# Pooled attention with a gated feed-forward block: weight words joined by VectorE, another product order in the scores, more movable operations, a new schedule

## The chip, the core and the metric

The kernel runs on one core of a Trainium2 chip. The metric is the device time of one launch in microseconds (us). TensorE (PE) multiplies, VectorE (DVE), ScalarE (ACT) and GpSimd (POOL) do the elementwise work, and SyncE (SP) issues the transfers.

## What is computed

```
q_pool = q.reshape(B, H, S // 2, 2, D).mean(axis=3)          # B,H,S,D = 4,8,1152,64
scores = (q_pool @ k.T) / sqrt(D)                            # 576 queries x 1152 keys
attn   = exp(scores - max);  attn /= attn.sum() + 1e-9
x      = (attn @ v), heads side by side                      # 4 x 576 x 512
h      = relu(x @ w_in)                                      # 512 -> 1024
c[s]   = conv_w[0]*h[s-1] + conv_w[1]*h[s] + conv_w[2]*h[s+1]
out    = (h * sigmoid(c)) @ w_out                            # 1024 -> 512
```

Everything is float32 outside; the three weights arrive as float64 and are put together from their 32-bit words on the chip.

## The kernel before

**Stages.** The 32 heads are worked in 16 pairs of two. Per pair the pooled queries stand in five blocks `d` of up to 128 rows (the last one holds 64 rows of each head and counts as one unit), so there are nine score units per pair and 144 in all. A unit is: three products into three PSUM banks (`scores`, L459: main 0 is 512 keys on the head's own half of the rows, main 1 512 keys on the other half with the turned queries `qd`, main 2 the 128 keys that are left), the row maximum by DVE (`top`, L471), the exponential by ACT (`expo`, L476, which also sums), the inverse of the sum (L489 or L493, then L499), and then the weights are split into two half-precision parts: `high` (L523 on ACT or L518 on POOL) and `low` (L526, DVE), which a transposing transfer (L539) turns. For seven heads (`X32`) there is no split: the rows are scaled (`norm`, L557 on ACT, L561 on POOL or DVE), turned by TensorE (L575) and copied out of PSUM by ACT (L580). There are two PSUM buffers for scores (`r_s`), so that the scores of a unit wait for the exponential of the unit two before.

After the units of a group of blocks come the values (`values`, L605 and L611), a copy out (L621), and another split (`high` L627 on ACT or L629 on POOL, `low` L634 on DVE). After four pairs, one batch, comes the feed-forward block: `feed` runs eight chunks of 128 columns, each a product of twelve matmuls (L695), a relu (L701, ACT), the first tap (`tap0`, L708 on ACT or L712 on POOL), two more taps (L719, DVE), a tanh (L725, ACT) and the gate (L729, DVE); `second` is the last product (L902 on split parts for three of the groups, else L908 and L914), copied out by ACT and stored.

**Weights.** Each of 17 blocks of weights passes through ACT `size` (L991), DVE `clamp` (L995), three DVE bit operations (L1004, L1009, L1013), ACT `rest` (L1019, which turns the low words into numbers), a DVE product (L1026) and an addition (L1028, DVE or POOL). The queries' two rows are summed by L303 and copied and turned by ACT (L306, L310).

**Order.** Every operation is a task with an engine, and some have an alternative engine (`alt`). Three tables at the head of the file say all: `ORDER` is the order in which the tasks are issued, `SWAPPED` names the tasks that run on their alternative, `SLOTS` gives every tile its buffer. Each engine works its own tasks strictly in that order; what it waits for are the results of the others.

## Time and profile before

| | us |
|---|---|
| median of the runs shown | 636.63 (636.33 to 636.86) |
| span of the profiled execution | 633.9 |
| TensorE busy | 583.3 |
| VectorE busy | 575.9 |
| ScalarE busy | 520.2 |
| GpSimd busy | 159.6 |

The span runs from the first to the last instruction of the profiled execution; 2.7 us of the median lie around it. Busy times are unions of the instructions' records. Records of one engine overlap by some hundredths of a microsecond, so that a sum of durations is a little larger than the union. A wait is named as "engine line <- what ended it".

### The profile page before, as it was taken

To read this page: it belongs to the slowest core of one execution; us is meant where nothing else is said; L and a number is where in the kernel's file an instruction comes from. 1 tells how busy PE (TensorE), PEld (TensorE's weight loads), DVE (VectorE), ACT (ScalarE), POOL (GpSimd) and SP (SyncE) were. 2 spreads that over 40 slices of the span, in tenths; PEclk is the share of its full clock that TensorE was granted. 3 is DMA by queue.
4 is the path that set the end of the run, shared out by engine and by line. 5 is a ranking of instruction groups with operands and counts; after the bars stand their busy time and mean duration, and the time that the engine had idled before them with its cause. 6 is when DMAs were issued, how large, how long until landed. Compare 5 with 4: busy or idle time off the path is not lost. (4 is left out here: it accounts for less than half of the span.)

```text
span 633.9 us, 11947 instructions
## 1 busy us (share of the span) xinstructions
PE 583.3 (92%) x4427; PEld 365.1 (58%) x4427; DVE 575.9 (91%) x948; ACT 520.2 (82%) x976; POOL 159.6 (25%) x166
## 2 busy tenths in 40 slices
PE   5679887898999899999999999999998999999997
PEld 3346554566665556546666666475665646566853
DVE  4999989999999999989998999999999999997771
ACT  5999989989998897879977899787869985775761
POOL 0332436533233312210212511202330122322210
PEclk7869989999999999999999999999999999999999
DMA  7788975847975599998989998999999898887601
GB/s 246 234 221 223 197 127 118 207 116 191 182 197 109 131 193 169 177 219 162 248 176 190 177 241 168 159 217 195 199 181 210 175 173 152 166 153 152 93 35 42
DMA packets 277386, 109.63 MB, mean 173 GB/s; under 512 B 264912, under 2 KB 266192, under 8 KB 277328
## 3 DMA queue, kind: packets, MB, share of 16 engines
q1 hardware_dynamic: 277328, 108.87, 83.3%
q8 instruction: 35, 0.57, 0.4%
q14 instruction: 23, 0.19, 0.1%
HBM read 37.77 MB, written 4.72 MB: 67 GB/s over the span
## 5 line engine op out<-in xcount | busy, mean ns | idle before, releaser
L476 ACT ACTIVATE p<-s,sm 128x1152 f32<-128x1152 f32 x144 | 175.2, 1217 | 41.2 <-DVE sm L471 18.8
L459 PE MATMUL s<-kt,qt 64*128 64x512 f32 (+3 forms) x704 | 189.0, 484 | 20.7 <-ACT p L476 16.5
L471 DVE TENSOR_REDUCE sm<-s 128x1 f32<-128x1152 f32 x144 | 193.1, 1348 | 7.3 <-PE s L459 6.9
L526 DVE SCALAR_TENSOR_TENSOR hl<-p,sm,hl 128x1152 f16<-128x1152 f32 (+1 forms) x116 | 167.0, 1449 | 4.3 <-POOL hl L518 2.4
L459 PEld LDWEIGHTS s<-kt,qt 64*128 64x128 f32 (+1 forms) x704 | 92.6, 178 | 124.3 <-issue 78.1
L459 PE MATMUL s<-kt,qd 64*128 64x512 f32 x256 | 147.3, 658 | 0.0
L518 POOL TENSOR_SCALAR hl<-p,sm 128x1152 f16<-128x1152 f32 (+1 forms) x52 | 72.1, 1388 | 230.1 <-DVE sm L499 145.8
L605 PE MATMUL a<-pt,v 128*64 128x256 f16 (+2 forms) x1566 | 119.8, 272 | 0.4 <-DVE v L399 0.4
L695 PE MATMUL a<-x,wi 128*128 128x257 f16 (+3 forms) x864 | 105.4, 274 | 3.6 <-ACT h L701 1.7
L605 PEld LDWEIGHTS <-v 128*64 128x64 f16 x1566 | 91.1, 110 | 10.2 <-issue 2.2
L695 PEld LDWEIGHTS <-wi 128*128 128x128 f16 x864 | 76.6, 98 | 30.3 <-issue 10.6
L523 ACT ACTIVATE hl<-p,sm 128x1152 f16<-128x1152 f32 (+1 forms) x64 | 79.4, 1249 | 12.3 <-DVE sm L499 9.1
L908 PE MATMUL a<-wo,g 128*128 128x512 f32 x160 | 74.7, 604 | 0.0
L719 DVE SCALAR_TENSOR_TENSOR g<-h,cw,g 128x255 f32<-128x255 f32 (+3 forms) x144 | 66.7, 482 | 4.1 <-ACT g L708 2.5
L575 PE MATMUL a<-ident,p 128*128 128x128 f32 (+1 forms) x315 | 49.1, 281 | 17.1 <-ACT pt L580 7.3
L611 PE MATMUL a<-pt,v 128*64 128x256 f32 (+1 forms) x252 | 64.1, 409 | 0.0
L575 PEld LDWEIGHTS a<-ident,p 128*128 128x128 f32 (+1 forms) x315 | 32.9, 144 | 31.1 <-ACT pt L580 10.1
L580 ACT ACTIVATE pt<-a 128x384 f32<-128x384 f32 (+2 forms) x98 | 44.6, 475 | 5.3 <-PE a L575 5.2
L701 ACT ACTIVATE h<-a,bs 128x257 f32<-128x257 f32 (+3 forms) x72 | 33.9, 472 | 14.3 <-PE a L695 9.4
L561 POOL TENSOR_SCALAR p<-p,sm 128x1152 f32<-128x1152 f32 (+1 forms) x20 | 28.1, 1408 | 69.0 <-DVE sm L499 42.9
L908 PEld LDWEIGHTS a<-wo,g 128*128 128x128 f32 x160 | 28.4, 190 | 28.8 <-issue 26.9
L611 PEld LDWEIGHTS a<-pt,v 128*64 128x64 f32 x252 | 33.4, 137 | 10.3 <-issue 0.7
(135 smaller groups left out, 648.8 us busy)
## 6 DMA issues: line engine op xcount, KB each, us to landing
qin<-in_q_dram SPq DMA_DIRECT2D x15, 640.0 KB, 4.6
kt<-in_k_dram SPq DMA_DIRECT2D x15, 576.0 KB, 5.0
vin<-in_v_dram SPq DMA_DIRECT2D x9, 576.0 KB, 4.4
g<-in_moe_w_in_dram SPq DMA_DIRECT2D x8, 512.0 KB, 4.6
w<-in_moe_w_out_dram SPq DMA_DIRECT2D x8, 512.0 KB, 4.2
out_dram<-o SPq DMA_DIRECT2D x16, 256.0 KB, 2.6
vin<-in_v_dram SPq DMA_DIRECT2D x7, 288.0 KB, 3.9
v<-in_v_dram SPq DMA_DIRECT2D x7, 288.0 KB, 4.1
```

The lines of the kernel that those rows point to most:

```text
L459: nc.tensor.matmul(out=w, lhsT=f, rhs=kk, start=True, stop=True)
L471: nc.vector.tensor_reduce(out=sm[:, e:e + 1], in_=runs(st[e]), axis=AX.XY, op=ALU.max, negate=True)
L476: nc.scalar.activation(out=p.tile().rearrange("p (a n) -> p a n", a=2), in_=runs(st[e]), func=AF.Exp, bias=sm[:, e:e + 1], scale=1.0, accu ...
L518: eng.tensor_scalar(out=hl[rows, 0], in0=ps_[e][rows], scalar1=sm[rows, 6 + e:7 + e], scalar2=1.0, op0=ALU.mult, op1=ALU.mult,)
L523: nc.scalar.activation(out=hl[rows, 0], in_=ps_[e][rows], func=AF.Copy, scale=sm[rows, 6 + e:7 + e])
L526: nc.vector.scalar_tensor_tensor(out=hl[rows, 1], in0=ps_[e][rows], scalar=sm[rows, 6 + e:7 + e], in1=hl[rows, 0], op0=ALU.mult, op1=ALU.s ...
L575: nc.tensor.transpose(w[:, (i - a1) * nq:(i - a1 + 1) * nq], ps_[e][rows, i * P:(i + 1) * P], ident[rows, rows])
L605: nc.tensor.matmul(out=to, lhsT=o.v[:, e, c, vc:vc + D], rhs=o.pt[y, e][:, hl * NC + c, 0:n], start=(c == 0 and j == 0), stop=(c == NC - 1 ...
L611: nc.tensor.matmul(out=to, lhsT=o.v[:, e, c].bitcast(F32), rhs=p32.rearrange("p (a n) -> p a n", a=NC)[:, c, 0:n], start=(c == 0), stop=(c ...
L695: nc.tensor.matmul(out=w[:, 0:n], lhsT=wi[:, a, j, f * P:(f + 1) * P], rhs=x.x[:, c, s0:s0 + n], start=(i == 0 and j == 0), stop=(i == 2 a ...
L719: nc.vector.scalar_tensor_tensor(out=c, in0=h[:, t:t + tok], scalar=cw[:, f, t:t + 1], in1=c, op0=ALU.mult, op1=ALU.add)
L908: nc.tensor.matmul(out=w.tile(), lhsT=g[f // 4][:, f % 4, c:c + P], rhs=wo[:, f, :], start=(f == 0), stop=(f == FC - 1),)
```

## The change

The products of a score unit are issued in the order main 2, main 1, main 0. `rest` is gone, and the product behind it reads the low words itself. Five kinds of tasks can now run on another engine: turning the queries, the copies L580 and L621 and the relu on DVE, the clamp on POOL. `ORDER`, `SLOTS` and `SWAPPED` are new (`SWAPPED` has 308 tasks instead of 176); some costs written beside tasks are other numbers, which are used for nothing at run time, and some tags are added.

```diff
         def scores(ends):
-            for main in (0, 1, 2):
+            for main in (2, 1, 0):
                 for e in ends:
...
-        def rest():
-            _, lo32, hi32, mm, a = parts()
-            nc.scalar.activation(
-                out=hi32.bitcast(F32), in_=lo32.bitcast(U32), func=AF.Copy, scale=2.0 ** -52
-            )
-
         def join(n, eng=None):
             _, lo32, hi32, mm, a = parts()
             if n == 0:
-                nc.vector.tensor_tensor(out=mm, in0=mm, in1=hi32.bitcast(F32), op=ALU.mult)
+                nc.vector.scalar_tensor_tensor(
+                    out=mm, in0=lo32.bitcast(U32), scalar=2.0 ** -52, in1=mm, op0=ALU.mult, op1=ALU.mult
+                )
...
-        def clamp():
+        def clamp(eng):
             _, lo32, hi32, mm, a = parts()
-            nc.vector.tensor_scalar(
-                out=mm, in0=mm, scalar1=F64_MIN, scalar2=F64_MAX, op0=ALU.max, op1=ALU.min
+            eng.tensor_scalar(
+                out=mm, in0=mm, scalar1=F64_MAX, scalar2=F64_MIN, op0=ALU.min, op1=ALU.max
             )
...
-        t = add("DVE", 0.08 + m / 1900.0, clamp, after=[t], uses=[tmp], port=True)
+        t = add("DVE", 0.08 + m / 1900.0, clamp, after=[t], uses=[tmp], port=True,
+                alt=("POOL", 0.15 + m / 1113.0, True))
...
-        t = add("ACT", act(m, 0.08), rest, after=[t], uses=both)
...
-        def turn_q(e, cols):
+        def turn_q(eng, e, cols):
             h, g = slice(D - D * e, P - D * e), slice(D * e, D * e + D)
+            if eng is not nc.scalar:
+                eng.tensor_scalar(
+                    out=o.qd.tile()[h, cols], in0=o.qin[g, 0, cols], scalar1=QSCALE, scalar2=1.0,
+                    op0=ALU.mult, op1=ALU.mult,
+                )
+                return
...
+                        if eng is nc.scalar:
+                            nc.scalar.activation(out=to, in_=src, func=AF.Copy)
+                        else:
+                            eng.tensor_copy(out=to, in_=src)
...
                         add("ACT", act((a2 - a1) * nq), keep, after=[t],
-                            uses=[w, pt])
+                            uses=[w, pt], alt=("DVE", 0.06 + (a2 - a1) * nq / 930.0, False))
...
-        t = add("ACT", act(n, 0.1), keep, after=[t] + o.one, uses=[w] + ([] if all(o.x32) else [o.vs]), takes=[xf])
+        t = add("ACT", act(n, 0.1), keep, after=[t] + o.one, uses=[w] + ([] if all(o.x32) else [o.vs]), takes=[xf],
+                alt=("DVE", dve(n) + 0.01, False))
...
-            t = add("ACT", act(n, 0.155 if halved else 0.085), relu, after=[t, xs[0].back], uses=[w, xs[0].bs], takes=[h])
+            t = add("ACT", act(n, 0.155 if halved else 0.085), relu, after=[t, xs[0].back], uses=[w, xs[0].bs], takes=[h],
+                    alt=None if halved else ("DVE", dve(n) + 0.01, False))
...
 ORDER = """
-hZcZcXaac1c4c0c5c6c7cYh0auc2bNc3abacaddcaededdc8afdbh3h1daagdfahc9h2dtaih4aviiajawh5aEaxdsaybOilh6h7azifijh8aA
...
+hIdXcIcGaacNcJcPcOcQcHashJcKabcRhKaccUcScMcThMadhLaecLafathNh1dbauaghOavahawh4aihPaxc0aBhQcVhYh2hRcWcZhZhUc1hV
...
```

What the tables do is seen in the order of each engine. How many tasks of a kind run where, before and after, is this:

| line before: task | engine | before | after |
|---|---|---|---|
| L995 clamp | DVE / POOL | 17 / 0 | 3 / 14 |
| L303 sum of queries | DVE / POOL | 15 / 3 | 3 / 15 |
| L561 norm (L557 on ACT) | DVE / POOL / ACT | 9 / 20 / 6 | 1 / 23 / 11 |
| L1028 addition | DVE / POOL | 9 / 8 | 5 / 12 |
| L493, L489 sum of a unit | DVE / ACT | 39 / 41 | 23 / 57 |
| L523, L518 high | ACT / POOL | 64 / 52 | 44 / 72 |
| L708, L712 first tap | ACT / POOL | 51 / 21 | 5 / 67 |
| L627, L629 high of x | ACT / POOL | 25 / 11 | 2 / 34 |
| L580 copy of a turned block | ACT / DVE | 98 / 0 | 85 / 13 |
| L310 turning queries | ACT / DVE | 36 / 0 | 29 / 7 |
| L701 relu | ACT / DVE | 72 / 0 | 65 / 7 |
| L621 copy of values | ACT / DVE | 36 / 0 | 33 / 3 |
| L1019 rest | ACT | 17 | 0 |

DVE at the start of the program, up to the first row maximum (L471 before, L480 after; L1029, L1034, L1038 are the bit operations L1004, L1009, L1013, and L304 and L312 sum and turn queries). Before:

```order
L995 TENSOR_SCALAR g<-g 128x512
L1004 TENSOR_SCALAR wo<-g 128x512
L303 TENSOR_TENSOR qin<-qin 128x384
L1009 SCALAR_TENSOR_TENSOR wo<-g,wo 128x512
L303 TENSOR_TENSOR qin<-qin 128x128
L1013 TENSOR_SCALAR g<-wo 128x512
L471 TENSOR_REDUCE sm<-s 128x1
L1026 TENSOR_TENSOR g<-g 128x512
```

After:

```order
L304 TENSOR_TENSOR qin<-qin 128x128
L312 TENSOR_SCALAR qd<-qin 64x128 x2
L304 TENSOR_TENSOR qin<-qin 128x128
L480 TENSOR_REDUCE sm<-s 128x1
L1029 TENSOR_SCALAR wo<-g 128x512
L1034 SCALAR_TENSOR_TENSOR wo<-g,wo 128x512
L1038 TENSOR_SCALAR g<-wo 128x512
L480 TENSOR_REDUCE sm<-s 128x1
```

The first row maximum has moved ahead of all weight work; before, four operations on weights stood in front of it.

PE at its last score units (L459 before, L467 after; L605 is a product with values, L902, after L927, a product of `second`). Before:

```order
L459 MATMUL s<-kt,qt 64x512 x4
L459 MATMUL s<-kt,qt 64x2x64 x2
L459 MATMUL s<-kt,qt 64x512 x4
L459 MATMUL s<-kt,qt 64x2x64 x2
L605 LDWEIGHTS v
L605 MATMUL a<-pt,v 64x256
```

After:

```order
L619 LDWEIGHTS v
L619 MATMUL a<-pt,v 64x256
L467 MATMUL s<-kt,qt 64x2x64 x2
L467 MATMUL s<-kt,qt 64x512 x4
L927 LDWEIGHTS kt
L927 MATMUL a<-w,kt 128x512
```

One product with values of 256 rows (54 matmuls) and three feed chunks of 257 columns (36 matmuls of L695) have moved from behind the last score to ahead of it; the other 570 matmuls behind it are the same.

POOL in the middle of the program (L518 before and L528 after are `high` of a unit, L712 and L736 first taps, L629 and L647 `high` of x). Before:

```order
L712 TENSOR_SCALAR g<-h,cw 128x255
L391 TENSOR_SCALAR v<-vin,vs 128x9x64
L561 TENSOR_SCALAR p<-p,sm 128x1152
L712 TENSOR_SCALAR g<-h,cw 128x321
L518 TENSOR_SCALAR hl<-p,sm 128x1152
L303 TENSOR_TENSOR qin<-qin 128x640
```

After:

```order
L528 TENSOR_SCALAR hl<-p,sm 128x1152 x2
L736 TENSOR_SCALAR g<-h,cw 128x255 x3
L528 TENSOR_SCALAR hl<-p,sm 128x1152
L736 TENSOR_SCALAR g<-h,cw 128x255 x2
L647 TENSOR_SCALAR x<-xf,bs 128x320
L736 TENSOR_SCALAR g<-h,cw 128x255
L304 TENSOR_TENSOR qin<-qin 128x640
```

The same kinds stand there, but almost twice as many of them in all.

## Rows read from the trace of the kernel before

**Rows 1.** Page part 1: busy us, share of span, instructions, by engine.

```profile
PE 583.3 (92%) x4427; PEld 365.1 (58%) x4427; DVE 575.9 (91%) x948; ACT 520.2 (82%) x976; POOL 159.6 (25%) x166
```

**Rows 2.** Busy us by stretch: PE, PEld, DVE, ACT, POOL; granted clock, DMA share, GB/s.

```profile
16.00:128.00 112.00, 91.37 (x587) 56.51 (x585) 106.24 (x179) 106.07 (x206) 45.78 (x42) 0.91 0.80 189
128.00:256.00 128.00, 119.44 (x911) 78.50 (x908) 125.12 (x195) 114.81 (x213) 34.15 (x33) 1.00 0.75 162
384.00:512.00 128.00, 123.76 (x944) 75.85 (x941) 123.21 (x189) 106.88 (x192) 22.40 (x25) 1.00 1.00 190
576.00:634.00 58.00, 53.07 (x583) 34.05 (x580) 34.70 (x98) 30.23 (x83) 7.89 (x11) 0.99 0.34 70
```

**Rows 3.** Waits: engine, line, waited for: us in total, times, longest.

```profile
ACT p L476 <- DVE sm L471: 18.8, 19, 3.2
...
PE s L459 <- ACT p L476: 16.5, 21, 1.6
```

**Rows 4.** Start, by time: start us, us, engine, line, [idle before <- what ended it].

```profile
8.45 0.43 DVE L995 TENSOR_SCALAR g<-g 128x512 f32<-128x512 f32 x1 [7.59 <-ACT g L991]
...
9.99 1.22 PE L459 MATMUL s<-kt,qt 64*128 64x512 f32 x1 [3.69 <-DMA kt<-in_k_dram]
...
10.87 1.35 DVE L471 TENSOR_REDUCE sm<-s 128x1 f32<-128x1152 f32 x1
```

**Rows 5.** DVE groups by form: count | busy us, mean ns | idle before.

```profile
L471 DVE TENSOR_REDUCE sm<-s 128x1 f32<-128x1152 f32 x144 | 193.1, 1348 | 7.3 <-PE s L459 6.9
...
L303 DVE TENSOR_TENSOR qin<-qin 128x640 f32<-128x640 f32 x13 | 10.6, 818 | 0.2 <-DMA qin<-in_q_dram 0.2
...
L561 DVE TENSOR_SCALAR p<-p,sm 128x1152 f32<-128x1152 f32 x5 | 4.1, 811 | 0.0
...
L995 DVE TENSOR_SCALAR g<-g 128x512 f32<-128x512 f32 x8 | 3.4, 421 | 8.1 <-ACT g L991 8.1
```

**Rows 6.** ACT groups by form: count | busy us, mean ns | idle before.

```profile
L523 ACT ACTIVATE hl<-p,sm 128x1152 f16<-128x1152 f32 x60 | 74.4, 1250 | 12.2 <-DVE sm L499 9.1 <-DMA pt<-hl 0.8 <-ACT g L708 0.7
...
L1019 ACT ACTIVATE w<-w 128x512 f32<-128x512 uint32 x8 | 5.4, 681 | 0.0
```

**Rows 7.** POOL by line: durations ns min/median/max, first and last start, forms.

```profile
L518 POOL TENSOR_SCALAR hl<-p,sm x52: 1223/1228/2507, 25.8 to 581.4; 128x1152 f16<-128x1152 f32 x49, 64x1152 f16<-64x1152 f32 x3
...
L712 POOL TENSOR_SCALAR g<-h,cw x21: 486/636/1540, 160.0 to 613.5; 128x255 f32<-128x255 f32 x13, 128x321 f32<-128x321 f32 x4, 128x256 f32<-128x256 f32 x3, 128x65 f32<-128x65 f32 x1
...
L303 POOL TENSOR_TENSOR qin<-qin x3: 456/1547/1722, 3.5 to 199.6; 128x640 f32<-128x640 f32 x2, 128x128 f32<-128x128 f32 x1
```

**Rows 8.** Middle, by time, DVE and then POOL: start us, us, what.

```profile
300.34 1.35 DVE L471 TENSOR_REDUCE sm<-s 128x1 f32<-128x1152 f32 x1
...
311.25 1.41 DVE L526 SCALAR_TENSOR_TENSOR hl<-p,sm,hl 128x1152 f16<-128x1152 f32 x1
...
300.29 1.23 POOL L518 TENSOR_SCALAR hl<-p,sm 128x1152 f16<-128x1152 f32 x1 [11.28 <-issue]
311.32 2.08 POOL L629 TENSOR_SCALAR x<-xf,bs 128x320 f16<-128x320 f32 x1 [9.79 <-ACT xf L621]
```

**Rows 9.** DVE low halves: the group's mean, and min/median/max.

```profile
L526 DVE SCALAR_TENSOR_TENSOR hl<-p,sm,hl 128x1152 f16<-128x1152 f32 x109 | 157.2, 1451 | 4.2 <-POOL hl L518 2.4 <-ACT hl L523 1.2
...
L526 DVE SCALAR_TENSOR_TENSOR hl<-p,sm,hl x116: 1399/1411/2699, 18.3 to 583.0; 128x1152 f16<-128x1152 f32 x109, 64x1152 f16<-64x1152 f32 x7
```

**Rows 10.** Chain that ended last, from 560 us: start us, us, what.

```profile
565.91 3.07 PE a L605 x54
...
571.67 1.32 PE a L695 x12
...
630.10 0.38 ACT o L928
```

**Rows 11.** The same chain: one score unit alone, and two in a row.

```profile
491.37 1.34 PE s L459 x6
...
422.60 2.14 PE s L459 x10
```

More of the change, by code (lines that the diff above doesn't have):

```diff
@@ L160 @@
+JPJRJTKuKBKIKPKWK3LaLhLsLwLDLKLRLYL5McMjMsMuMxMyMFMMMTMZM0M6M7NeNl
 """
@@ L319, in loads @@
             ready = [tq] + [
-                add("ACT", act(turned.stop - turned.start, 0.16), lambda e=e, turned=turned: turn_q(e, turned), after=[t],
-                    uses=[o.qin] + ([o.qd] if e or i else []), takes=[] if e or i else [o.qd]) for e in range(2)
+                add("ACT", act(turned.stop - turned.start, 0.16), lambda eng, e=e, turned=turned: turn_q(eng, e, turned), after=[t],
+                    uses=[o.qin] + ([o.qd] if e or i else []), takes=[] if e or i else [o.qd],
+                    alt=("DVE", 0.08 + (turned.stop - turned.start) / 1900.0, True)) for e in range(2)
             ]
@@ L466, in softmax @@
         for e in range(n):
+            plan.tag = ('softmax', o.pr, d, 2 if m else e)
             p = Buf(r_p)
@@ L550, in softmax @@
                     continue
+                plan.tag = ('softmax', o.pr, d, h)
                 pt = o.pt[y, h]
@@ L564, in norm @@
                     )
-                td = add("POOL", 1.28, norm, after=[iv], uses=[sm, ps_[e]] + ([] if new else [pt]),
+                td = add("POOL", 1.22, norm, after=[iv], uses=[sm, ps_[e]] + ([] if new else [pt]),
                          takes=[pt] if new else [], port=True,
-                         alt=("ACT", act(S, 0.1), False) if d % 2 else ("DVE", 0.08 + S / 1900.0, True))
+                         alt=("ACT", act(S, 0.1), False) if d % 2 else ("DVE", 0.12 + S / 1900.0, True))
                 groups = ((0, 5), (5, 9)) if m else ((0, 3), (3, 6), (6, 9))
@@ L618, in values, with keep @@
         to = slice(1 + first, 1 + first + n)
[L620 to L623 removed]
+        def keep(eng):
+            by = 2.0 ** -14 if all(o.x32) else o.vs[:, 4:5]
+            if eng is not nc.scalar:
+                eng.tensor_scalar(
+                    out=xf[:, 0:n], in0=w[:, 0:n], scalar1=by, scalar2=1.0, op0=ALU.mult, op1=ALU.mult
+                )
+                return
+            nc.scalar.activation(out=xf[:, 0:n], in_=w[:, 0:n], func=AF.Copy, scale=by)
         def high(eng):
@@ L698, in mm, with relu @@
                         )
-            def relu(f=f, w=w, h=h):
+            def relu(eng=nc.scalar, f=f, w=w, h=h):
+                if eng is not nc.scalar:
+                    eng.tensor_scalar(
+                        out=h[:, 0:n], in0=w[:, 0:n], scalar1=xs[0].bs[:, 3:4], scalar2=0.0, op0=ALU.mult, op1=ALU.max
+                    )
+                    return
                 nc.scalar.activation(
```

140 lines of the change are left out of this document (69 added, 71 removed).

## The prediction

> **What bounds the kernel now.** I read the busy times first [rows 1]: TensorE 583.3 us and VectorE 575.9 us of a span of 633.9 us. Neither fills it, so the stretches come next [rows 2], and there the reader is to see that the bound is not one engine. From 16 to 128 us DVE is busy 106.24 and ACT 106.07 of 112 us, and PE only 91.37: the weights are joined there beside the first softmaxes. From 128 to 256 DVE has 125.12 of 128. From 384 to 512 DVE (123.21) and PE (123.76) are level, and the transfers are busy all the time (1.00). From 576 on PE has 53.07 of 58 and DVE 34.70. So DVE sets the pace until the last softmax, shared with ACT at first and with PE later, and what is left then is a tail of matmuls. The waits agree [rows 3]: ACT's exponential waits 18.8 us for DVE's row maximum, and TensorE's scores 16.5 us for the exponential that frees their PSUM buffer. Third, the chain that ended last [rows 10]: from 565.9 us, where the last score unit ends, it is TensorE without a gap worth the name, until the last copy out at 630.1.
>
> The time is therefore made of two pieces: when the last score unit runs, which hangs on DVE's order up to the third-last row maximum (two score buffers), and the matmuls behind that unit.
>
> **DVE's work.** Removed, with durations of [rows 5]: 14 clamps x 0.42 = 5.9 us (16 of 512 columns, one small one, 3 stay); 13 query sums of 640 columns x 0.82, less one of 128 more at 0.29, = 10.4; 8 scalings at 0.81 or a little more = 6.5 to 7.5; four additions of 512 columns at 0.69 (the sum of 640 at 818 ns, less 128 columns at 1.04 ns, the slope between the rows of 640 and of 1152) = 2.7; 16 sums of two columns at 0.15 (the row maximum's 1348 ns less 1152 x 1.04) = 2.5. Together about 28.5. Added: 13 copies of turned blocks from PSUM, 7 relus, 3 copies of values, 7 query turns. DVE copies nothing out of PSUM in this trace; the nearest row is the row maximum, 1152 PSUM columns in 1348 ns, which gives 0.5 us for 384 columns, and I take that (bounds 0.4, as if in SBUF, to 0.6): 13 x 0.5 + 7 x 0.35 + 3 x 0.3 + 7 x 0.35 = 12.3. The joining product keeps its price: two inputs of 512 columns before and after; that it now reads unsigned words has no row of its own on DVE, and ACT's row for that conversion, 681 ns [rows 6], is no longer than DVE's two-input pass, so 0, bounds -1 to +3 us for all 17. Net over the program: -16.
>
> What counts is what stands ahead of the third-last row maximum. Going through both orders with these durations: 27.6 us of the removals and 11.2 of the additions lie ahead of it, and 4.3 us that stood behind it have been moved ahead of it (five taps, two gates, two low halves of x, one of a unit, less one long split). That is -12.1, with 18 instructions fewer; since records overlap by 0.07 us or so, -10.9.
>
> **The start.** DVE's first row maximum starts at 10.87 us [rows 4], though its scores were done at 9.99 - 3.69 = 6.30: in DVE's order four weight operations stand ahead of it, the first of which waits for ACT until 8.45. In the new order only the sums and turns of the first queries are ahead. The first maximum can start some 4 us sooner; the second one needs the second part of the keys, which landed at 9.99 and is issued one transfer (0.6 us) earlier. I take 3 us for DVE (bounds 1 to 4.4).
>
> **ACT.** It loses 17 `rest` at 0.68 [rows 6] = 11.5, 20 high halves at 1.25 = 25, 46 first taps and 23 high halves of x at about 0.5 = 35, and some 11 more: from 520 to about 437. In the first 256 us it was as full as DVE, so this must accompany DVE's relief there, or that would be worth nothing. By itself I give it 2 us (bounds 0 to 6): exponentials that stand behind other ACT work come sooner.
>
> **POOL, and the wait that is added.** All this goes to POOL. With undisturbed times, the minima of [rows 7]: 20 more halves x 1.23 = 24.6, three scalings 3.7, 12 query sums x 1.55 = 20.7 less a short one, 46 taps x 0.5 = 23, 23 halves of x x 0.5 = 12, 14 clamps at 0.7 (between 0.49 for 255 columns and 1.23 for 1152) = 9.8, others 14: 108 us on top of some 137 (159.6 as recorded, with waits in it). An engine that is busy 40% is no bound by itself. But [rows 8] show what it costs: a POOL half of a unit beside a row maximum takes 1.23; a POOL operation on 320 columns that starts with DVE's 1.41 us low half takes 2.08, where short operations take 0.49 undisturbed. POOL waited for DVE. The other way round, [rows 9] have DVE's low halves at 1451 ns on average, 1411 in the median and up to 2699: 109 x 0.04 = 4.4 us lost; they are 167 of some 358 us of DVE's two-input and fast work (575.9 less 193 of maxima and 25 of tiny operations), so in all between 4.4 and 9.4, I take 7.5. Queued behind such an operation are the row maxima, and behind these the exponentials and the scores. Scaled by POOL's work (245 / 137) this grows by 6 us; scaled by its square, by 16. Nothing excludes less, if the order puts POOL beside the maxima, which take 193 us; I take +6, bounds 0 and 16.
>
> If POOL could run beside none of that DVE work, 358 - 26 + 245 = 577 us would have to follow one another in some 617; before, 358 + 137 = 495 in 634. It fits, but with little room, which is the first rival below.
>
> The Trainium skill (SBUF — State Buffer, "Who interferes with whom") gives the rule: DVE and GpSimd share one port pair under an exclusive lock, an operation with two SBUF inputs or in a two-port mode holds it for its whole length, and a reduction never needs it. It speaks against this change, and the trace agrees: 2.08 us against 1.23 beside a maximum. By the rule the sum just made would be a hard floor, 577 us, under the forecast; so the rule alone changes the chance of the rival and not the sum.
>
> **128 keys first.** A unit alone takes 1.34 us on TensorE, two in a row 2.14 [rows 11]. The columns on each half of the rows are the same in either order, so I take 0. Bounds: the short product first may hide a weight load of 0.1 us per unit or expose one more: -13 to +13 over 128 units, of which only those count where TensorE is the bound.
>
> **The tail.** Ahead of the last score now stand one product with values (54 matmuls, 3.07 us in [rows 10]) and three feed chunks (3 x 1.32 to 1.43): 7.1 us less behind it. TensorE must have done these 7.1 us earlier, beside DVE's work; it idles 50.6 us in the span, nearly all before 576, so there is room.
>
> **The sum**, against the execution profiled: 633.9 - 10.9 (DVE) - 3 (start) - 2 (ACT) + 6 (POOL in DVE's way) + 0 - 7.1 (tail) = 616.9. With the 2.7 us that lie between span and median (636.6 - 633.9): 619.6, say **620 us**. Its own range, with start, POOL and ACT at their bounds but not all on one side: 611 to 630.
>
> **Rivals.**
> *POOL and DVE in each other's way.* For: the two together fill 94% of the span by the sum above, and DVE's two-input operations often stand back to back. Against: before, POOL's 137 us cost DVE only 7.5 (5%). If 20% of POOL's 245 us comes back as DVE waiting, that is 49 instead of 7.5, and the time is 636.6 - 16 - 7.1 + 41.5 - 0 = 655; at 14% it is 640. It decides from 12% on (30 us), where the gain is gone: slower.
> *TensorE and the transfers hold the middle.* From 384 to 512 us PE is at 97% and the transfers at 1.00 [rows 2]; DVE's relief there buys nothing. Then of the 10.9 only the 5.8 before 128 us count: 636.6 - 5.8 - 3 + 3 - 7.1 = 627.
> *More than the sum.* ACT is no longer full beside DVE. If half of TensorE's 50 us of idle time goes instead of a third, and the stretch at the lower clock at the start shrinks (0.91 granted from 16 to 128, between the levels of 1.2 and 2.4 GHz), then 606.
> *The score order costs.* If each unit gets 0.1 us longer where TensorE is the bound, the forecast turns to 633.
>
> **How the numbers follow.** The forecast 0.50, POOL against DVE 0.17, the held middle 0.15, more than the sum 0.13, the score order 0.05. A measurement of this kernel can tell 0.2% from no change, here 635.3 to 637.9. Faster: 0.49 + 0.15 + 0.13 + 0.02 = 0.79; within: 0.04, from the score order and the light end of the first rival; slower: 0.17. The range must leave out no more than 2 in 10: 604 leaves out part of the fourth case, about 0.05, and 639 most of the first rival, about 0.14.
>
> **What would show it.** After, DVE busy should be near 560 and ACT near 440, POOL 270 to 330 as recorded, with the median of its halves still 1.23. The first row maximum should start at 6.5 to 7.5 us, the last score unit end at 554 to 562 (565.9 now), and the chain behind it hold 57 us of TensorE. The mean of DVE's low halves tells the first rival: 1.45 to 1.50 us by the forecast, 1.65 and more if POOL is in the way. Two units in a row on TensorE should stay at 2.14. I am wrong in mechanism if the last score unit is not earlier although DVE's work ahead of it shrank; then DVE's idle time tells whether it waits for POOL's results, which would be a wait that I have priced at nothing.

## The result, and the profile after

The changed kernel takes **641.39 us** (median of 14 runs, 637.14 to 646.84), the kernel before 636.53 in the same comparison: ratio 1.0078, interval 1.0058 to 1.0097. It is **0.8% slower**, where 2.6% faster was forecast. The profiled execution has a span of 639.9 us, against 633.9 before. TensorE's granted clock does not make the difference. At the same mean clock over a whole run, 0.976 (a mean between its levels of 1.2 and 2.4 GHz), the runs on record of the kernel before take 636.3 to 638.3 us and those of the changed kernel 639.7 to 644.3. Within the runs of the changed kernel the time does go with the clock (637.1 and 639.9 us at 0.981, 645.0 at 0.970); what drives what there is not shown.

Page part 1 of the changed kernel (busy us, share of the span, instructions), and under it the busy us by stretch, as in [rows 1, 2]:

```profile
PE 582.2 (91%) x4427; PEld 353.5 (55%) x4427; DVE 590.3 (92%) x924; ACT 450.0 (70%) x853; POOL 275.8 (43%) x296
```

```profile
16.00:128.00 112.00, 92.57 (x615) 55.50 (x615) 108.63 (x172) 105.00 (x197) 47.88 (x50) 0.91 0.83 191
128.00:256.00 128.00, 119.24 (x883) 73.84 (x879) 122.82 (x185) 104.92 (x190) 58.76 (x59) 0.97 0.77 165
384.00:512.00 128.00, 118.10 (x881) 69.76 (x882) 120.28 (x180) 75.77 (x145) 53.78 (x54) 1.00 0.92 177
576.00:640.00 64.00, 57.09 (x598) 34.62 (x592) 42.78 (x106) 24.00 (x59) 19.49 (x32) 1.00 0.44 85
```

ACT was relieved by 70 us, and POOL took 116 us more. But DVE, which lost 24 instructions and was to lose 16 us, is busy **14.4 us longer**. Where that time sits is seen in DVE's groups by form (columns as in [rows 5]), and in the low halves' minimum, median and maximum:

```profile
L480 DVE TENSOR_REDUCE sm<-s 128x1 f32<-128x1152 f32 x144 | 192.0, 1345 | 7.2 <-PE s L467 6.6
L536 DVE SCALAR_TENSOR_TENSOR hl<-p,sm,hl 128x1152 f16<-128x1152 f32 x109 | 166.1, 1532 | 4.6 <-POOL hl L528 3.7 <-ACT hl L533 0.2
L743 DVE SCALAR_TENSOR_TENSOR g<-h,cw,g 128x255 f32<-128x255 f32 x64 | 32.8, 534 | 0.6 <-ACT g L732 0.5
L652 DVE SCALAR_TENSOR_TENSOR x<-xf,bs,x 128x256 f16<-128x256 f32 x20 | 13.4, 670 | 2.0 <-POOL x L647 2.0
...
L536 DVE SCALAR_TENSOR_TENSOR hl<-p,sm,hl x116: 1398/1409/2743, 17.1 to 598.4; 128x1152 f16<-128x1152 f32 x109, 64x1152 f16<-64x1152 f32 x7
```

The row maxima (L480, 1345 ns) are as they were (1348 in [rows 5]). The low halves have the same median (1409, and 1411 in [rows 9]) and a mean that rose from 1451 to 1532: most are untouched, and some are twice as long. One such place, by time, DVE and POOL:

```profile
320.96 2.85 POOL L528 TENSOR_SCALAR hl<-p,sm 128x1152 f16<-128x1152 f32 x2 [6.16 <-DVE sm L508]
...
321.56 1.36 DVE L480 TENSOR_REDUCE sm<-s 128x1 f32<-128x1152 f32 x1
322.83 2.18 DVE L536 SCALAR_TENSOR_TENSOR hl<-p,sm,hl 128x1152 f16<-128x1152 f32 x1
```

POOL makes two halves in a row. The row maximum beside the first takes its usual 1.36 us. The low half at 322.83 starts while POOL is in its second half, and takes 2.18 instead of 1.41.

**A count over all records.** For each form at each line of DVE I took the duration at the lower quarter as undisturbed, and added up what instructions exceed it by (if over 60 ns), where they ran beside a POOL instruction. I call this DVE's lengthening. Before it was 8.4 us in 14 instructions, after **39.5 us in 64**: 13.5 in the low halves, 8.3 in the taps L743, 5.9 in the input's low parts L652, the rest scattered. By what POOL did meanwhile: 12.3 beside high halves, 10.9 beside query sums, 4.1 beside taps. Without it DVE would have 550.8 us after and 567.5 before: its own work did shrink, by 16.7 us as forecast. The places where the two meet explain part of it: before, 97.5 of POOL's 162.1 recorded us lay beside row maxima, which aren't lengthened; after, 143.1 of 280.2. So POOL's time beside the rest of DVE's work went from 63 to 139 us. That is 2.2 times as much, while the lengthening became 4.7 times as much: this time alone doesn't give the size either, and the experiments go down to single instructions.

The exponential's wait for row maxima grew as well, from the 18.8 us of [rows 3]. The first three lines are of after: the exponential's wait, and what the weight loads and the matmuls of TensorE's scores wait for exponentials. The last line is of before, for the weight loads, which [rows 3] doesn't have:

```profile
ACT p L485 <- DVE sm L480: 43.3, 32, 3.9
...
PEld s L467 <- ACT p L485: 37.5, 47, 2.4
...
PE s L467 <- ACT p L485: 13.0, 20, 1.5
...
PEld s L459 <- ACT p L476: 35.2, 54, 1.9
```

Weight loads and matmuls of the scores together waited 51.7 us before (35.2 and 16.5) and wait 50.5 now, so TensorE waits no longer than it did. Nor is ACT's longer wait a measure of the loss: ACT has 70 us less of its own to do, and in e11 below, where the lengthening is back to 9.2 us, the same wait is still 31.4.

### The profile page after: what moved, and what is told of

Read it like the earlier page. It is cut to its first block, busy times and chain, and to the rows that moved or that the text cites. A ratio compares the mean times of both kernels' runs of the same rounds, so it can differ in the third digit from the quotient of the medians.

```text
span 639.9 us, 11934 instructions
## 1 busy us (share of the span) xinstructions
PE 582.2 (91%) x4427; PEld 353.5 (55%) x4427; DVE 590.3 (92%) x924; ACT 450.0 (70%) x853; POOL 275.8 (43%) x296
## 4 chain that ended last, share of the span: by engine, by line
DVE 41%; PE 32%; ACT 9%; issue 8%; DMA 5%; POOL 4%; SPq 0%; ACTq 0%; POOLq 0%; DVEq 0%
DVE hl L536 12%; DVE sm L480 12%; PE s L467 9%; PE a L714 6%; PE a L933 5%; DVE g L743 5%; PE a L619 5%; ACT p L485 4%; DMA pt<-hl 4%; PE a L927 3%; DVE g L753 2%; PE a L625 2%; PE a L587 1%; DVE x L652 1%; POOL hl L528 1%
## 5 line engine op out<-in xcount | busy, mean ns | idle before, releaser
L480 DVE TENSOR_REDUCE sm<-s 128x1 f32<-128x1152 f32 x144 | 192.0, 1345 | 7.2 <-PE s L467 6.6
L467 PE MATMUL s<-kt,qt 64*128 64x128 f32 (+2 forms) x704 | 186.1, 480 | 13.4 <-ACT p L485 13.0
L536 DVE SCALAR_TENSOR_TENSOR hl<-p,sm,hl 128x1152 f16<-128x1152 f32 (+1 forms) x116 | 176.0, 1525 | 4.7 <-POOL hl L528 3.7
L467 PE MATMUL s<-kt,qd 64*128 64x512 f32 x256 | 148.6, 662 | 2.9 <-DMA kt<-in_k_dram 2.9
L528 POOL TENSOR_SCALAR hl<-p,sm 128x1152 f16<-128x1152 f32 x72 | 94.8, 1321 | 129.5 <-DVE sm L508 81.7
L467 PEld LDWEIGHTS s<-kt,qt 64*128 64x128 f32 (+1 forms) x704 | 79.6, 179 | 62.7 <-ACT p L485 37.5
L743 DVE SCALAR_TENSOR_TENSOR g<-h,cw,g 128x255 f32<-128x255 f32 (+3 forms) x144 | 73.3, 533 | 7.2 <-POOL g L736 6.5
L736 POOL TENSOR_SCALAR g<-h,cw 128x255 f32<-128x255 f32 (+3 forms) x67 | 49.1, 738 | 68.0 <-ACT h L725 49.9
L533 ACT ACTIVATE hl<-p,sm 128x1152 f16<-128x1152 f32 (+1 forms) x44 | 54.9, 1249 | 11.0 <-DVE sm L508 8.1
L573 POOL TENSOR_SCALAR p<-p,sm 128x1152 f32<-128x1152 f32 (+1 forms) x23 | 31.6, 1373 | 45.6 <-DVE sm L508 41.4
L725 ACT ACTIVATE h<-a,bs 128x257 f32<-128x257 f32 (+3 forms) x65 | 30.9, 480 | 25.4 <-PE a L714 13.5
L596 ACT ACTIVATE pt<-a 128x384 f32<-128x384 f32 (+2 forms) x85 | 38.7, 475 | 8.9 <-PE a L587 8.5
## 6 DMA issues: line engine op xcount, KB each, us to landing
kt<-in_k_dram SPq DMA_DIRECT2D x15, 576.0 KB, 4.7
vin<-in_v_dram SPq DMA_DIRECT2D x9, 576.0 KB, 4.6
```

Of the source, the lines that this page charges most:

```text
L467: nc.tensor.matmul(out=w, lhsT=f, rhs=kk, start=True, stop=True)
L480: nc.vector.tensor_reduce(out=sm[:, e:e + 1], in_=runs(st[e]), axis=AX.XY, op=ALU.max, negate=True)
L528: eng.tensor_scalar(out=hl[rows, 0], in0=ps_[e][rows], scalar1=sm[rows, 6 + e:7 + e], scalar2=1.0, op0=ALU.mult, op1=ALU.mult,)
L533: nc.scalar.activation(out=hl[rows, 0], in_=ps_[e][rows], func=AF.Copy, scale=sm[rows, 6 + e:7 + e])
L536: nc.vector.scalar_tensor_tensor(out=hl[rows, 1], in0=ps_[e][rows], scalar=sm[rows, 6 + e:7 + e], in1=hl[rows, 0], op0=ALU.mult, op1=ALU.s ...
L743: nc.vector.scalar_tensor_tensor(out=c, in0=h[:, t:t + tok], scalar=cw[:, f, t:t + 1], in1=c, op0=ALU.mult, op1=ALU.add)
```

## The experiments

A table of the runs first. "Rest" is the span less DVE's busy time; the measuring stage (e10) has a section of its own.

| kernel | time us | ratio to before (interval) | DVE busy | rest | lengthening | ACT busy |
|---|---|---|---|---|---|---|
| before | 636.5 | 1 | 575.9 | 58 | 8.4 | 520 |
| changed | 641.4 | 1.0078 (1.0058 to 1.0097) | 590.3 | 50 | 39.5 | 450 |
| e1 all high halves on ACT | 656.4 | 1.0308 (1.0286 to 1.0330) | 575.0 | 78 | 20.6 | 530 |
| e2 feed and input on ACT | 648.8 | 1.0182 (1.0165 to 1.0199) | 589.0 | 59 | 37.2 | 491 |
| e3 query sums on DVE | 640.3 | 1.0057 (1.0033 to 1.0081) | 590.8 | 48 | 29.0 | 450 |
| e4 halves written, not read | 632.3 | 0.9932 (0.9910 to 0.9954) | 573.4 | 56 | 22.4 | 449 |
| e5 18 that lengthen, on ACT | 637.8 | 1.0025 (1.0010 to 1.0041) | 575.6 | 58 | 23.7 | 467 |
| e6 old engines, new order | 670.2 | 1.0523 (1.0501 to 1.0545) | 590.1 | 79 | 26.2 | 511 |
| e7 before, join alone | 636.9 | 1.0010 (0.9996 to 1.0024) | 576.0 | 60 | 9.1 | 512 |
| e8 before, score order alone | 636.3 | 1.0002 (0.9990 to 1.0014) | 576.4 | 57 | 9.2 | 520 |
| e9 before, more POOL work | 675.0 | 1.0620 (1.0605 to 1.0636) | 600.2 | 73 | 32.4 | 523 |
| e11 second pass | 628.5 | 0.9892 (0.9874 to 0.9909) | 569.4 | 57 | 9.2 | 470 |
| e12 control: 18 others on ACT | 644.0 | 1.0110 (1.0084 to 1.0135) | 588.3 | 54 | 37.5 | 470 |

### The small parts alone: joining, and the order of the score products

The kernel before, with the joining changed (e7) and with the products reversed (e8):

```diff
         def rest():
-            nc.scalar.activation(
-                out=hi32.bitcast(F32), in_=lo32.bitcast(U32), func=AF.Copy, scale=2.0 ** -52
-            )
+            pass
...
-                nc.vector.tensor_tensor(out=mm, in0=mm, in1=hi32.bitcast(F32), op=ALU.mult)
+                nc.vector.scalar_tensor_tensor(
+                    out=mm, in0=lo32.bitcast(U32), scalar=2.0 ** -52, in1=mm, op0=ALU.mult, op1=ALU.mult
+                )
```

```diff
-            for main in (0, 1, 2):
+            for main in (2, 1, 0):
```

> The kernel before with one part of the change alone: the 17 ACT instructions that scale the low words are gone and DVE's multiplication takes the low words itself. ACT has 17 x 0.5 = 8 to 9 us less; DVE's 17 multiplications take the same time or up to 0.2 us more each. By the prediction's term for ACT (2 us gained): 634 to 636. If the removed ACT work was off the path: 636.5 within 1. If the multiplication with integer words is slower: up to 640.

> The kernel before with the 128-key products issued first in each unit, the order of the large products reversed, and nothing else. Prediction's term: 0 (bounds plus and minus 13 us). Theory (row maxima wait for the last product of a unit either way): 636.5 within 1.5. Rival (the order costs DVE's or ACT's start in a unit): 640 to 649; or a gain of some us.

Both are nothing: 1.0010 and 1.0002, both intervals with 1 in them. ACT lost 8 us by e7 (520.2 to 512.4) and the time did not follow; DVE's product with the low words costs no more (DVE 575.9 and 576.0). So the loss lies in the moved instructions, or in the new order and the buffers that go with it.

### Undoing parts: query sums, high halves, feed

Each is the changed kernel, with a loop ahead of the order that sets engines back (for e1 the tag is "softmax", for e2 "feed" and "values", to ACT):

```diff
+        for t in self.tasks:
+            if t.tag[0] == "loads" and t.engine == "POOL" and t.alt and t.alt[0] == "DVE":
+                t.engine = "DVE"
```

> The changed kernel with the 12 query sums that it moved from DVE to POOL back on DVE. DVE has about 10.4 us more of its own work, and loses about 10.9 us of lengthening that the trace shows beside the sums on POOL. Theory (POOL takes from DVE what it relieves it of): no difference, 641 within 4 us, DVE's busy time the same within 5. Rival (DVE is full with its own work alone): about 651.

> The changed kernel with one part undone: the 72 high halves of weights that it gave to POOL are back on ACT (94.8 us of POOL's recorded work; ACT has 90 us more, about 540 us). Theory (POOL and DVE are in each other's way: in the changed kernel's trace DVE's instructions are longer than their undisturbed like by 39.5 us in sum while POOL runs, 12.3 us of that beside these halves): DVE's lengthening falls by about 12 us and the time by 8 to 12, to 629 to 633. Rival (DVE is simply full with its own work, and POOL doesn't lengthen it): the low halves stay at a mean of 1525 ns and the time stays within 3 us of 641 or rises, since ACT has become fuller. Second rival (the new order is what costs): no gain either.

> The changed kernel with the feed's and the input's POOL work that ACT could do (67 taps, 3 split highs, 34 high parts of the input) back on ACT. By the overlap in the changed kernel's trace these lengthen DVE by 7 to 8 us in sum. Theory (POOL lengthens DVE): time about 634, DVE's lengthening near 32 us. Rival (ACT's own queue sets the end once it is fuller): 641 or more, with the row maxima waiting no less.

e3 went as the theory said, though its edit moves 15 sums and not the 12 of its text: all that POOL had, two of which lay on POOL before the change too. DVE took back 11 us of its own work (550.8 to 561.8 without lengthening) and is busy as long as in the changed kernel (590.8 and 590.3), since the lengthening fell by 10.5 us. On POOL these sums cost DVE what they cost on DVE. The rival's 651 is out.

e1 and e2 missed. The lengthening fell in e1 by 19 us and in e2 by 2, and both times rose. For e2 the rival's 641 or more came true; e1 rose as its rival allowed, but with low halves back at 1432 ns, which that rival excluded. Both undo more than the change did, which their texts don't say: of halves, taps and input parts POOL has 72, 67 and 34 now, and had 52, 21 and 11 before. Part of what e1 lost instead is in DVE's group of low halves, before which DVE sat idle 4.7 us in the changed kernel, 3.7 of it for POOL:

```profile
L539 DVE SCALAR_TENSOR_TENSOR hl<-p,sm,hl 128x1152 f16<-128x1152 f32 (+1 forms) x116 | 165.5, 1432 | 13.4 <-ACT hl L536 12.2
```

The mean is 1432 ns, nearly that of an undisturbed half, but DVE now waits 12.2 us for halves that stand in ACT's queue. "Rest" went from 50 to 78 us; of these 28 us the low halves have 9, row maxima wait 5 us more for scores, and the others are spread. So taking work from POOL is no cure in itself; that it depends on what ACT's queue can hold at that place is likely, but was not separated.

### Does POOL's reading do it?

POOL's 72 high halves become a constant: the part left out is the reading and the product, and the weights of these rows lie wholly in their low halves.

```diff
                 def high(eng, e=e, hl=hl, rows=rows):
                     if eng is not nc.scalar:
+                        eng.memset(hl[rows, 0], 0.0)
+                        return
```

> The changed kernel, but POOL's 72 high halves of weights are written as a constant zero and nothing is read (the part left out: these rows' weights then lie wholly in their low halves). POOL's access ends within some hundred ns instead of 1.2 to 1.3 us. If POOL's holding of the memory port is what lengthens DVE, about 12 us of DVE's 39.5 us lengthening go, as with the halves on ACT, but with no work added to ACT: 627 to 632. If DVE isn't lengthened by POOL, or if only POOL's writing counts, the low halves' mean stays near 1525 ns and the time stays at 641 within 4.

Page part 1, and the low halves:

```profile
PE 577.7 (92%) x4427; PEld 354.4 (56%) x4427; DVE 573.4 (91%) x924; ACT 449.1 (71%) x853; POOL 258.4 (41%) x296
...
L538 DVE SCALAR_TENSOR_TENSOR hl<-p,sm,hl 128x1152 f16<-128x1152 f32 x109 | 154.6, 1426 | 4.2 <-POOL hl L528 2.4 <-ACT hl L535 1.3
```

The same 72 instructions at the same places on the same engine, POOL busy nearly as long (258 and 276), and DVE is 17 us shorter, the low halves at 1426 ns, the time at 632.3, under the kernel before. By the count, 2.8 us of lengthening lie beside these 72 instructions, 12.3 in the changed kernel. So it is the reading that costs, together with the product that was left out with it; no run separates the two. The time gained 9 us and just missed the 627 to 632 that were expected. One detail of the expectation was wrong: a write of 1152 columns still takes POOL about 1.06 us, not some hundred ns, so that POOL's work lay beside the low halves as much as in the changed kernel (49 us in both).

### The disputed cost by itself

The kernel before, with a measuring stage ahead of it: six instructions of a kind on DVE, alone, then beside six high halves on POOL, then beside twelve writes.

```diff
+        for beside_it in ("nothing", "reads", "writes"):
+            for kind in kinds:
...
+                for _ in range(6):
+                    if beside_it == "reads":
+                        half()
+                    elif beside_it == "writes":
+                        nc.gpsimd.memset(lc[:, 0], 0.0)
+                        nc.gpsimd.memset(lc[:, 1], 0.0)
+                for _ in range(6):
+                    dve(kind)
```

> The kernel before with a measuring stage ahead of it: six at a time, the low-half form (two SBUF operands), the row-maximum form (reads PSUM) and a product with one SBUF operand in f32 on DVE, first with POOL idle, then beside six of POOL's high halves, then beside POOL writing constants. If POOL's reads keep DVE from SBUF: the low half rises from about 1.41 us to 2.0 to 2.7 us, the row maximum stays at 1.34 us, the one-operand product rises too; beside plain writes all stay within 0.1 us. If it's a matter of every access: the row maximum and the runs beside writes rise as well.

Its stage by time (start us, us for all six): low half L259, row maximum L264, product of one SBUF operand L269, POOL's halves L274. First alone, then beside reads, then beside writes.

```profile
6.08 8.61 DVE L259 SCALAR_TENSOR_TENSOR hl<-p,sm,hl 128x1152 f16<-128x1152 f32 x6
...
14.61 8.31 DVE L264 TENSOR_REDUCE sm<-s 128x1 f32<-128x1152 f32 x6
22.84 5.09 DVE L269 TENSOR_SCALAR p<-p,sm 128x1152 f32<-128x1152 f32 x6
...
27.96 13.07 DVE L259 SCALAR_TENSOR_TENSOR hl<-p,sm,hl 128x1152 f16<-128x1152 f32 x6
...
29.40 12.72 POOL L274 TENSOR_SCALAR hl<-p,sm 128x1152 f16<-128x1152 f32 x6
...
41.12 8.32 DVE L264 TENSOR_REDUCE sm<-s 128x1 f32<-128x1152 f32 x6
...
42.22 7.83 POOL L274 TENSOR_SCALAR hl<-p,sm 128x1152 f16<-128x1152 f32 x6
...
49.62 9.68 DVE L269 TENSOR_SCALAR p<-p,sm 128x1152 f32<-128x1152 f32 x6
...
50.67 9.71 POOL L274 TENSOR_SCALAR hl<-p,sm 128x1152 f16<-128x1152 f32 x6
...
59.34 9.52 DVE L259 SCALAR_TENSOR_TENSOR hl<-p,sm,hl 128x1152 f16<-128x1152 f32 x6
...
68.96 8.31 DVE L264 TENSOR_REDUCE sm<-s 128x1 f32<-128x1152 f32 x6
```

Beside reads six low halves take 13.07 us instead of 8.61; the first of them ran before POOL's halves began, so the other five take (13.07 - 1.42) / 5 = 2.33 each. POOL's halves go from 1.23 (its minimum) to (12.72 - 1.23) / 5 = 2.30. The two take turns: one low half and one high half, 1.42 + 1.23 = 2.65 us of work, in 2.3 us, so that only some 0.3 us of them overlaps. Row maxima are untouched (8.31 and 8.32), and POOL beside them too. The one-operand product rises from 5.09 to 9.68. Beside writes five of six low halves are undisturbed, and so are the row maxima. The 0.9 us that the group of low halves has too much belongs to its first, which starts at 59.34, while the last of POOL's high halves of the row before runs until 60.38. Here the expectation missed: the product of one operand, which was to keep its time beside writes, does not (17.59 us for six; the lines are in the last section).

The Trainium skill (SBUF — State Buffer, "Who interferes with whom") says that a DVE instruction with two SBUF inputs contends with a GpSimd instruction that reads SBUF and not with one that only writes, and that a reduction never does. This stage agrees in all three: 2.33 against 1.42, 1.42 beside writes, 1.36 for the maximum, which here reads PSUM.

### Load or place?

The kernel before in its own order, with 128 products that nobody needs: two of 512 columns from a constant, for each half that stays on ACT.

```diff
+                    for _ in range(2):
+                        nc.gpsimd.tensor_scalar(
+                            out=spare[rows].rearrange("p (a n) -> p a n", n=P), in0=ident[rows, None, :].to_broadcast([rows.stop - rows.start, 4, P]),
+                            scalar1=sm[rows, 6 + e:7 + e], scalar2=1.0, op0=ALU.mult, op1=ALU.mult,
+                        )
                     nc.scalar.activation(out=hl[rows, 0], in_=ps_[e][rows], func=AF.Copy, scale=sm[rows, 6 + e:7 + e])
```

> The kernel before, with its order and assignment, plus POOL work that nobody needs: for each of the 64 halves that stay on ACT, POOL waits for the same inverse sums and makes two products of 128x512 from a constant into a spare tile (128 instructions, some 70 to 80 us of reading work, so POOL's load is near that of the changed kernel, about 235 us). No other engine waits for them; POOL's own work can stand behind them by up to 1.2 us. By the prediction's term (lengthening in proportion to POOL's load, 6% of 75 us): DVE's lengthening 8 to 13 us, time 637 to 641. Theory now (there is room for POOL under the row maxima, which read PSUM and aren't lengthened, and before had filled it with its own 97 us; what comes on top falls beside SBUF-only work at 25 to 35%): lengthening 25 to 35 us, time 648 to 660. Rival (the loss in the changed kernel is its order, not POOL's load): 637 to 640 with lengthening under 15.

Page part 1, and two groups of DVE:

```profile
PE 597.6 (89%) x4427; PEld 371.4 (55%) x4427; DVE 600.2 (89%) x948; ACT 522.9 (78%) x976; POOL 297.1 (44%) x294
...
L472 DVE TENSOR_REDUCE sm<-s 128x1 f32<-128x1152 f32 x144 | 192.9, 1346 | 14.5 <-PE s L460 14.3
L532 DVE SCALAR_TENSOR_TENSOR hl<-p,sm,hl 128x1152 f16<-128x1152 f32 x109 | 166.1, 1530 | 9.7 <-POOL hl L519 8.5 <-ACT hl L529 0.6
```

The lengthening is 32.4 us, within the 25 to 35 of the theory and four times the 8.4 of before; the low halves' mean is 1530 ns, just that of the changed kernel. DVE's busy time rose by 24.3. The time rose by 39: more than expected, since the products took 1.02 us each on average instead of 0.6 (130 us, not 75; the shortest took 0.69), and POOL's own halves stood behind them, for which low halves waited 8.5 us (2.4 in [rows 9]). So more work on POOL, in the old order and with the old engines, makes a lengthening as large as that of the changed kernel. Of the 39 us of time 24 are DVE's, and the others are waits.

Then the other way round: new order, old engines for all 264 moved instructions.

```diff
-        for i in unpack(SWAPPED):
+        for i in set(unpack(SWAPPED)) ^ set(unpack(BACK)):
```

> The changed kernel's order, score order and joining of the low words, but every one of the 264 instructions that the change gave to another engine is back on its engine of before (POOL 296 to about 166 instructions, ACT near 500 us). Theory (the loss is POOL beside DVE, the order itself costs nothing): about 625 to 633, DVE's lengthening near 10 us. Rival (an order is worked out for one assignment; ACT's queue now holds instructions at places meant for POOL): 645 to 660, with a DVE lengthening as low as 10 us, as when ACT got the 72 halves.

670.2 us, the rival's direction and beyond its range. And the lengthening did not fall to 10 us: with POOL's old load of 137 us undisturbed, it is 26.2. Two groups of DVE show part of the waits, 21 us; "rest" is 79 us, against 58 before and 50 in the changed kernel:

```profile
L545 DVE SCALAR_TENSOR_TENSOR hl<-p,sm,hl 128x1152 f16<-128x1152 f32 (+1 forms) x116 | 169.6, 1469 | 12.0 <-ACT hl L542 7.8 <-POOL hl L537 3.1
...
L517 DVE RECIPROCAL sm<-sm 128x2 f32<-128x2 f32 (+1 forms) x80 | 12.7, 159 | 8.9 <-ACT sm L507 8.3
```

DVE waits here mostly for ACT, in whose queue instructions now stand at places that were worked out for POOL. So neither load nor order is the cause by itself alone: the old order had 60% of POOL's time beside row maxima, and its 137 us of work cost 8.4 us; either change, more load (32.4) or another order (26.2), spoils that.

### A handful of instructions, and a control

If place is what counts, a few instructions must hold most of the loss. In the changed kernel's trace 32 POOL instructions each lengthen DVE by over 600 ns, 32.2 us in sum. e5 gives ACT 18 of them, 16.5 us in sum (the other 14 are nine query sums, three scalings and two additions); e12 gives ACT 18 others of POOL, of the same kinds and from nearly the same places, beside which DVE shows no lengthening.

```diff
+        back = set(unpack(BACK))
         for i in unpack(SWAPPED):
+            if i in back:
+                continue
             t = self.tasks[i]
             t.engine = t.alt[0]
```

> The changed kernel with 18 of POOL's 296 instructions moved to ACT: those (13 high halves, 2 of the feed's high parts, 3 others, nearly all after 255 us) beside which the changed kernel's trace shows a DVE instruction lengthened by over 600 ns, 16.5 us of the 39.5 us in sum. ACT gets about 23 us more (450 to 473 of 640). Theory (POOL's reads beside DVE's SBUF-only instructions are the loss, and they are few): DVE's lengthening falls to 23 to 27 us, the time to 627 to 632, below the kernel before. Rival (what ACT gets in its queue costs more than POOL's lengthening, as when all 72 halves went there and the time rose to 656): 641 or more. Third case: other POOL work slides under the same DVE instructions: lengthening stays above 33 us, time 638 to 642.

> The control to the run in which 18 instructions that lengthened DVE went to ACT (637.8 us, lengthening 23.7 us): 18 others of POOL go to ACT, of the same kinds (14 high halves, 2 of the split, 1 of the input's, 1 tap) and nearly the same places, beside which the changed kernel's trace shows no lengthening of DVE at all. Theory (it counts which POOL instructions lie beside SBUF-only work, not how many there are): the lengthening stays at 35 to 45 us, and the time at 641 or above, up to 646 by ACT's fuller queue. Rival (any 18 instructions less on POOL help alike): lengthening about 24 to 30 us and 636 to 639.

Page part 1 and the low halves, of e5 and then of e12:

```profile
PE 579.5 (91%) x4427; PEld 353.3 (56%) x4427; DVE 575.6 (91%) x924; ACT 467.3 (74%) x871; POOL 250.6 (40%) x278
...
L544 DVE SCALAR_TENSOR_TENSOR hl<-p,sm,hl 128x1152 f16<-128x1152 f32 x109 | 158.4, 1461 | 6.2 <-POOL hl L536 3.5 <-ACT hl L541 2.1
```

```profile
PE 582.4 (91%) x4427; PEld 353.8 (55%) x4427; DVE 588.3 (92%) x924; ACT 469.5 (73%) x871; POOL 253.3 (39%) x278
...
L544 DVE SCALAR_TENSOR_TENSOR hl<-p,sm,hl 128x1152 f16<-128x1152 f32 x109 | 161.7, 1490 | 5.6 <-ACT hl L541 3.4 <-POOL hl L536 1.4
```

POOL and ACT are equally busy in both, and DVE is 12.7 us apart: 23.7 us of lengthening against 37.5. The right 18 bring 637.8, the wrong 18 bring 644.0. Which instructions lie on POOL decides, and not how many. The size was off, though: 14.7 us of DVE's busy time saved 3.6 us of time, not 9 to 14. "Rest" grew by 9 of them (49.6 to 58.3), and the execution profiled is 2.1 us faster than e5's median.

The second pass applies the rule to e5's trace. Twelve POOL instructions that lengthen DVE by more than DVE needs to do them go to DVE, and two go to ACT (a high half and the high part of a weight block).

```diff
+        for i in unpack(ON_DVE):
+            self.tasks[i].engine = "DVE"
+        for i in unpack(ON_ACT):
+            self.tasks[i].engine = "ACT"
```

> The changed kernel with the 18 instructions on ACT as before, and a second pass of the same rule on that run's trace: 12 of POOL's instructions that lengthened DVE by more than DVE itself needs for them (7 query sums, 1.16 to 1.34 us lengthening against 0.8 us; 2 weight joins, 3 weight products) go to DVE, 2 halves to ACT. DVE's lengthening falls by about 13 us to 10 or 11, its own work rises by 9: net 4 us. Theory: 632 to 635, under the kernel before. Rival (other POOL work slides to the same places): 637 to 639, no gain on the 637.8 of the first pass.

Page part 1 and the low halves:

```profile
PE 580.0 (93%) x4427; PEld 355.0 (57%) x4427; DVE 569.4 (91%) x936; ACT 469.5 (75%) x873; POOL 230.2 (37%) x264
...
L552 DVE SCALAR_TENSOR_TENSOR hl<-p,sm,hl 128x1152 f16<-128x1152 f32 x109 | 155.7, 1436 | 6.4 <-POOL hl L544 3.6 <-ACT hl L549 2.1
```

**628.5 us**, 1.1% under the kernel before (0.9892, 0.9874 to 0.9909), about 2% under the changed kernel. DVE does 12 instructions more and is busy 6.2 us less: the lengthening is down to 9.2 us, that of the kernel before, with 197 us of POOL's work instead of 137. Nothing that costs as much slid into the places that came free. It is better than expected (632 to 635). So 32 of the 296 POOL instructions (18 picked in one trace and 14 in the next) made the difference between a change that loses and one that wins.

## Why the prediction was wrong

**The step that failed is one term: POOL in DVE's way, +6 us with bounds 0 and 16.** By the lengthening it was 39.5 - 8.4 = +31. Put in its place, the sum gives 633.9 - 10.9 - 3 - 2 + 31 - 7.1 = 641.9 against a span of 639.9. That this fits so well is in part luck: with the start and the tail as measured below (2.3 and 5.2) and nothing for ACT it would be 646.5, so that some 6 us of the lengthening didn't become time, or another term was larger than could be seen.

Three choices made the term small. The earlier cost, 7.5 us, was right (8.4 by the count). It was then scaled by POOL's load, by 245 / 137, and its upper bound by the square; POOL's undisturbed work did come out at 236 (the sum of its parts has a slip: 12 query sums at 1.55 are 18.6 and not 20.7, which makes 243 of the 245). But e9 and e6 show that the cost does not follow the load. Before, 60% of POOL's time lay under row maxima, where it is free; the rate of 6% (8.4 of 137) was that of one particular order, and what the new order does with the added work couldn't be read from it. The text had the rule, the row of 2.08 against 1.23, and the remark that row maxima might hide the work, and used them for a floor of 577 us of things that can't overlap, and for a rival. It did not do what could have told: count, in the order of the changed kernel, which POOL instructions stand beside row maxima and which beside low halves and taps. e10 gives the price of one meeting, 0.9 us for each half beside a low half, so that some 35 such meetings are enough.

**The rival that came true** is the first, POOL and DVE in each other's way, at 0.17. Its share was 39.5 / 236 = 17%, between its 14% (640) and 20% (655), and by its own formula the time would be 636.6 - 16 - 7.1 + 32 = 645.5; measured 641.4. Its turning point was 12%, 30 us in all (22 more than the 7.5), and the 39.5 us measured lie beyond it, on the losing side. The mark set for it (a mean of the low halves of 1.65 us and more; 1.45 to 1.50 for the forecast) was badly chosen: the mean is 1.53, since only 13.5 of the 39.5 us fell on low halves. DVE's busy time was the mark that told: about 560 was forecast, 590.3 measured. And I asked whether DVE would wait idle for POOL's results, while the loss came as busy time.

**The other steps.**
- DVE's own work: -16 forecast, -16.7 by the count (567.5 to 550.8). Right.
- ACT: 437 us forecast, 450.0 measured; its own term, -2 us, is 0 where a part of it can be seen alone (e7: 8 us of ACT less, of some 70; 1.0010).
- Score products: 0, and 0 measured (e8). The two units in a row still take 2.14 us, as in [rows 11].
- The start: the first row maximum was to start at 6.5 to 7.5 us and starts at 8.61; the second at 11.40. DVE's order put a query sum ahead of it that waits for a transfer:

```profile
8.40 0.29 DVE L304 TENSOR_TENSOR qin<-qin 128x128 f32<-128x128 f32 x1 [4.14 <-DMA qin<-in_q_dram]
8.61 1.35 DVE L480 TENSOR_REDUCE sm<-s 128x1 f32<-128x1152 f32 x1
...
11.40 1.35 DVE L480 TENSOR_REDUCE sm<-s 128x1 f32<-128x1152 f32 x1
```

 That is 2.3 us sooner than in [rows 4], where the sum took 3 (bounds 1 to 4.4). The transfer was not looked at in the sum.
- The last score unit was to run at 554 to 562 us and ends at 577.1 (the first line below), 11 us later than the 565.9 of [rows 10]. This is the lengthening up to there: 27 us more than before, against 16 us of relief (the terms for DVE, the start and ACT).
- The tail: 62.8 us lie behind that unit, against 68.0 before, so 5.2 of the 7.1 us came. The last row maximum starts only at 586.26 us, 9 us behind the last score unit; before it was 1 us (566.94 and 565.9). The chain that ended last runs through DVE up to there, and then has a transfer of turned weights in it ahead of the feed:

```profile
575.81 1.29 PE L467 MATMUL s<-kt,qt 64*64 64x128 f32 x12
...
586.26 1.35 DVE L480 TENSOR_REDUCE sm<-s 128x1 f32<-128x1152 f32 x1
...
588.75 4.75 DMA pt<-hl
594.55 5.47 PE a L714 x48
...
623.34 9.06 PE a L927 x42
632.41 3.63 PE a L939 x32
```
- The second rival's sum, 636.6 - 5.8 - 3 + 3 - 7.1, is 623.7 and not 627. It is 18 us under the measured time either way.

**What stays open.** DVE's busy time doesn't give the time by itself: e4 and e5 have nearly the same (573.4 and 575.6) and lie 5.5 us apart, and e5 gained 3.6 us and e11 another 9.3 for 14.7 and 6.2 us of DVE (6.0 and 7.8 us between the executions profiled). Nor does the time that POOL spends beside DVE's work other than row maxima give the lengthening: e11 has 90 us of it and 9.2 of lengthening, the kernel before 63 and 8.4. That ACT's fuller queue takes part of it is likely by e1 and e6, but was not separated. Whether the new order would do better had it been worked out with the price of a meeting in it was not tried.

## What to carry to other kernels

When work goes to an engine that shares a path with the bound one, price it by its neighbours and not by its load: here a POOL instruction was free beside a row maximum that reads PSUM and cost DVE 0.9 us beside a low half, which has two SBUF operands (both of 1152 columns), and 32 of 296 made the sign. Compare each instruction's duration with the lower quarter of its own form, list those beside which the bound engine is longer, and move only these (to a third engine with room, or back, where the lengthening is more than the work itself). An order that has been worked out for one assignment may be worth nothing with another: here the new order with the old engines took 670 us.
